# Attention output of the first batch repeated and added on TensorE, with a re-planned order of casts, copies and pooled V

## The chip, the core and the metric

The kernel runs on one core of one Trainium2 chip. The metric is the device time of one execution in microseconds (us); lower is better. Before the change the median of four runs is 338.2 us (336.63 to 339.19).

## What is computed

Two steps in one launch: an "hourglass" attention on q, k, v of shape (8 batches, 8 heads, 576 tokens, 64), and a feed-forward on its output.

```python
q_d, k_d, v_d = (mean over groups of 4 tokens)       # 144 tokens
out_d  = softmax(q_d @ k_d.T / 8) @ v_d
out_up = np.repeat(out_d, 4, axis=2)                 # back to 576 tokens
local  = softmax over |i - j| < 4 of q @ k.T / 8, times v
x = (out_up + local).transpose(0, 2, 1, 3).reshape(4608, 512)
h = x @ w_in                                         # (512, 2048)
out = (h - np.tanh(h)) @ w_out                       # (2048, 512), float32
```

## The kernel before, in words

**Pairs and groups.** The unit of attention is a pair of heads of one batch (`attention(p)`, 32 pairs, p = 0 to 31, four to a batch); q and k are loaded and turned for two pairs at a time (group n = p // 2). The unit of the dense part is a block of 512 tokens (kb, nine of them): 16 steps of `mm1` (h of 128 features: four matmuls L739, tanh on ACT L748, subtraction to gT on DVE L751), then `mm2` (gT times w_out, L794, copied out by ACT L805). One batch is 576 tokens, so block 0 can begin once all four pairs of batch 0 are in xT: each mm1 step reads xT of all four.

**A group on its way in.** DMA brings q and k to `qkn` (L372). `reorder` casts them to bf16 `qr` (L477). `turn` transposes on TensorE (nine transposes, L505, into a PSUM tile) and copies to `qk` (L514). Two additions make the pooled q and k (L518 to `half`, L523 to `qkd`). V comes to `vst` (L398) and is cast to `vw` (L435); `pool_v` pools V of a group with six matmuls by a 0/1 matrix `pick` (L453, L455) and ACT copies it to `vd` (L460).

**A pair.** Local scores come in 120-column tiles: s1 (L572) and s2 (L572 and, for the pooled scores, L591). In batch 0 the mask is added in PSUM first by a matmul with the identity (L566). ACT takes the exps to E (L608, L634, L637); later batches multiply by the mask on DVE (L612, L641). `outs` makes both outputs with their sums (L652 local, L658 pooled). DVE takes reciprocals (L669) and normalises to `ln` (L671). For p < 12 TensorE transposes `ln` back: two transposes of the pooled part (L706, L707) and five of the local part (L710), all bf16 into PSUM. ACT copies the pooled part to `od` (L713), and DVE adds local and repeated pooled part into xT (L715). From p = 12 on a DMA transposes `ln` to `lnT` and DVE adds (L691).

**PSUM.** `ps_ts` and `ps_ox` serve attention. While batch 0 is in the works, the even pairs have a second set, `ps_ts1` and `ps_ox1`; these banks become the four `ps_hy` of the dense part.

**Order.** Nothing runs in the order of the code. Each `op` is recorded with an engine, a cost, its reads, writes and a priority; `choice` leaves the engine open. `Program.order()` lays all of them out by a list schedule, and `emit` issues them in that order, so each engine's queue is fixed when the kernel is built. In it come the constants near the end: which engine casts what (`CV`, `RE`, `TU`, `AD`, `CAST`), which copies and additions are split in two halves (`TS`, `AS`), in which PSUM set a group is turned (`TB`), where a group's turning and V pooling is placed (`PLACE`, `PV`), priorities (`LATE`, `URG`), margins between engines (`LATER`, `SPARE`), how far loads run ahead (`AHEAD`), and the order of the weight loads (`ORDER`: g is the load of the next group, 0 to 3 are quarters of w_out). SyncE (SP) issues all DMAs in one queue: q, k, v of batch 0, the four quarters of w_in, group 2, then group 3 and w_out. Weights are staged as float32 and cast (L426).

**Fillers.** Where the plan shows TensorE idle for over 350 ns before the first dense step, `emit` puts in matmuls of a zero tile `warm` (L1006), as many as 0.75 of the gap divided by an assumed duration (`slow`).

Of the kernel before, what the change touches and what calls it, by code (L numbers as in the profile page):

```python
# [9 lines left out]
BF16 = mybir.dt.bfloat16  # L10
AF = mybir.ActivationFunctionType
ALU = mybir.AluOpType
# [3 lines left out]
class Program:  # L16
# [127 lines left out]
    def emit(self, banks=None, end=None, filler=None):  # L144
        order = self.order()
        fill = {}
        if filler:
            until = min(self.start[i] for i in range(len(self.ops)) if end in self.touch[i])
            self.uses = {name: sorted(
                (self.start[i], self.start[i] + self.ops[i][1] + 200, i in self.fresh)  # L150
                for i in range(len(self.ops)) if self.touch[i] & set(keys))
                for name, keys in banks.items()}
            for i, name, room in self.idle(order, banks, until):
                slow = 430 if self.start[i] < 6000 else 230
                fill[i] = (name, int(0.75 * room / slow))
        for i in order:
            if i in fill:
                filler(*fill[i])
            if self.ops[i][2] is not None:
                self.ops[i][2]()  # L160
# [3 lines left out]
def kernel(  # L164
# [10 lines left out]
    B, H, S, D = q.shape  # L175
# [10 lines left out]
    QW = 120  # L186
    NT = 5
# [22 lines left out]
    warm = fixed("warm", [128, 512], BF16)  # L210
# [40 lines left out]
    P = Program()  # L251
# [6 lines left out]
    LATER = 160  # L258
# [29 lines left out]
    def c_bias():  # L288
# [3 lines left out]
        for part, pat in ((m4, [[0, 4], [1, QW]]),  # L292
# [13 lines left out]
            fill=OFF, base=99, pattern=[[0, 96]], channel_multiplier=-1)  # L306

# [50 lines left out]
    def load_qk(n):  # L358

        b, h0, s = n // 2, 4 * (n % 2), slot_qk(n)  # L360
        for i, src in enumerate((q, k)):
            P.put(n, ("qkn", s, i))
            for y in range(2):
# [7 lines left out]
                def issue(to=to, rows=rows):  # L371
                    nc.sync.dma_start(out=to, in_=rows)  # L372
                load(650, issue, [("qkn", s, i, y)],
                     T_QK + (400 if n == 0 and i == 1 else 0), -30,
# [66 lines left out]
    def pool_v(hb):  # L441
# [6 lines left out]
        bank, key = (ps_ox1, "ox1") if hb == 0 else (ps_ox, "ox")  # L448
        pv = bank[:, 0, :].rearrange("p (w c) -> p w c", w=2)

        def mm():
# [8 lines left out]
        op("ACT", 600, lambda: A.copy(  # L460
            out=vd[w][:, :, :, 0:64],
            in_=pv.rearrange("p w (h d) -> p w h d", d=D)),
# [8 lines left out]
    def reorder(n, i):  # L471
        s, sn = n % 2, slot_qk(n)
        P.has(n, ("qkn", sn, i))
        P.put(n, ("qr", s, i))
        dst = qr[s][:, i].rearrange("p a (x d) -> p x a d", d=D)
        srt = qkn[sn][:, i].rearrange("p x (a d) -> p x a d", d=D)
        P.choice([(eng, ns, lambda fn=fn: fn(out=dst, in_=srt))  # L477
                  for eng, ns, fn in REORDER[RE.get((n, i), 3 + i)]],
                 reads=[("qkn", sn, i, x) for x in range(2)],
                 writes=[("qr", s, i)], pri=20 * n - 12)  # L480

    def turn(n, i):
# [7 lines left out]
        pri, cold = 20 * n, (1.5 if n < 1 else 1.0)  # L490
        b16 = ps.rearrange("p n c -> p (n c)").bitcast(BF16)[:, 0:A6 * 128]
        if n >= FI:
# [6 lines left out]
               reads=[("qr", s, i)], writes=ts + [("q", ("qT", i))], pri=pri - 60)  # L499
            op("DMA", T_IN, None, reads=[("q", ("qT", i)), ("qr", s, i)], writes=ts,  # L500
# [5 lines left out]
        if n < FI:  # L506
            P.fresh.add(len(P.ops))
            op("PE", 480 * cold, tr, reads=[("qr", s, i), "ident"], writes=ts, pri=pri)
# [40 lines left out]
    def attention(p):  # L549
# [97 lines left out]

        def outs():
# [29 lines left out]

        if p >= XOUT:
# [6 lines left out]
            xo = xT[j][:, b * S:(b + 1) * S]  # L686
# [14 lines left out]


# [23 lines left out]
    def mm1(kb, fc):  # L726
# [15 lines left out]
        for part in range(2):  # L742
# [3 lines left out]
               [("x", b, j) for b in bs for j in dcs],  # L746
# [66 lines left out]
    def dense(kb):  # L813
# [18 lines left out]
        if kb == NBLK:  # L832
# [4 lines left out]
    XOUT, T_OUT, AHEAD = 12, 1600, 6  # L837
    P_A, LATE = 5000, {0: 26, 1: 5, 2: 25, 3: 25}
    MERGE, GV = 12, 7
    FI, T_IN = 11, 2050  # L840
    XADD = [("DVE", (800, 350), V)]
    ORDER, W_FIRST = 'g0123', '0123qv'
    TB = {(1, 0), (1, 1), (2, 0), (3, 0)}
    PV = {2: -1, 3: 0, 4: 1, 5: 0, 6: 0}
    PLACE = {2: (2, 4), 3: (1, 3), 4: (4, 4), 5: (0, 2), 6: (2, 3), 7: (1, 1), 8: (0, 3)}
    W_LATE = [300, 1400, 0, 0]
    T_QK, T_V, T_W, W_PRI = 900, 780, 2750, 33
# [5 lines left out]
    CV = {0: 0, 1: 0, 2: 3, 3: 1, 4: 1, 5: 0, 6: 0, 7: 3, 8: 1, 9: 0, 10: 2, 11: 1}  # L853
# [4 lines left out]
    RE = {(0, 0): 4, (0, 1): 4, (1, 0): 4, (1, 1): 4, (2, 0): 1, (2, 1): 0, (3, 0): 3, (3,  # L858
          1): 4, (4, 0): 3, (4, 1): 4, (5, 0): 1, (5, 1): 1}
# [3 lines left out]
    TU = {(0, 0): 0, (0, 1): 0, (1, 0): 1, (1, 1): 0, (2, 0): 0, (2, 1): 0, (3, 0): 0, (3,  # L863
          1): 0, (4, 0): 2, (4, 1): 1, (5, 0): 2, (5, 1): 0}
# [6 lines left out]
    TS, AS = {(0, 0): 1, (1, 1): 3, (4, 0): 3}, {(0, 1): 3, (1, 1): 3}  # L871
    URG = {'e1': {4: -2, 5: -2, 6: -2, 7: -2}, 'od': {4: -2, 5: -2, 6: -2, 7: -2}, 'norm':
          {8: -2, 9: -2, 10: -2, 11: -2}, 'add': {4: -2, 5: -2, 6: -2, 7: -2}, 'turn': {4:
          -2, 5: -2}}
    ADDERS = [[("DVE", 760, 440, V), ("POOL", 1190, 850, GP)],
              [("POOL", 1190, 880, GP)], [("DVE", 760, 440, V)]]
    AD = {(0, 0): 0, (0, 1): 1, (1, 0): 0, (1, 1): 2, (2, 0): 1, (2, 1): 0, (3, 0): 0, (3,
          1): 0, (4, 0): 1, (4, 1): 0, (5, 0): 0, (5, 1): 2}
# [5 lines left out]
    op("POOL", 500, c_mask, reads=["bias"], writes=["mask"], pri=20)  # L884
# [82 lines left out]
    for hb in range(2):  # L967
        pool_v(hb)
    for p in range(NPAIR):
# [14 lines left out]
        if p % 2 == 0 and 1 < n < GV and PV.get(n, 0) == 1:  # L984
            pool_v(n)
        next(work[p], None)
# [17 lines left out]
    def filler(name, n):  # L1004
        for _ in range(n):
            T.matmul(tiles[name][:, 0, :], warm[:, 0:128], warm, start=True, stop=True)  # L1006
# [31 lines left out]
```

## Time and profile before

The profiled execution took 339.19 us, of which 337.5 us are the span from first to last instruction; it is the slowest of the four.

| what | us |
|---|---|
| TensorE busy, of 337.5 | 319.7 |
| DVE, ACT, POOL busy | 238.3, 207.6, 149.1 |
| first dense matmul (L739) | 27.16 |
| dense matmuls without a break from | 30.49 |
| first mm2 matmul (L794) | 51.88 |
| mean granted TensorE clock, 0 to 20, 20 to 30, 30 to 40, 40 to 50 us | 1.00, 0.81, 0.68, 1.00 |
| last matmul ends | 334.5 |

Lines of the timeline give start, length, engine, source line, operation, output and inputs with shapes, how many in a row, and in brackets the idle time before and what ended it. PE is TensorE, SPq the DMA-issuing queue of SyncE. In rows of windows a number in brackets counts instructions. The granted clock is a share of full speed. Durations of matmuls include their passage through the array; what counts in a row of matmuls is their distance.

### The profile page before, as it was taken

The numbers are of one execution on the slowest core, as the hardware profiler recorded it, in microseconds if no ns is written. First come the engines' busy times: TensorE is split into PE (matmuls) and PEld (weight loads), VectorE is DVE, ScalarE is ACT, GpSimd is POOL, SyncE is SP. The second block draws the span as 40 slices with busy tenths as digits, with TensorE's granted clock in tenths as the row PEclk, the third lists the DMA queues.
The fourth block names the chain that finished last, engine by engine and source line by source line (L and its number), as shares of the span: only waits on it lengthen the run. The fifth ranks groups of instructions, "written<-read, shape, count | busy, mean of one in ns | idle before, by whom it ended". The sixth has DMA issues, their size and how long they took to land.

```text
span 337.5 us, 6713 instructions
## 1 busy us (share of the span) xinstructions
PE 319.7 (95%) x2522; PEld 165.5 (49%) x2565; DVE 238.3 (71%) x385; ACT 207.6 (62%) x337; POOL 149.1 (44%) x168
## 2 busy tenths in 40 slices
PE   6687999999999999999999999999999999999996
PEld 2363445555555555545444545444444444444444
DVE  3986799789996898799787887898665443343300
ACT  2574688558777767485959794958754344344421
POOL 8642196187389268986664776473200000000000
PEclk9995899999999999999999999999999999999999
DMA  6999999899920599999999999993124100100012
GB/s 199 248 383 321 281 337 325 226 291 231 316 74 33 105 234 271 223 256 206 252 220 242 211 270 228 254 223 83 63 61 79 40 33 31 62 33 32 31 65 94
DMA packets 96878, 60.47 MB, mean 179 GB/s; under 512 B 74510, under 2 KB 80078, under 8 KB 96846
## 3 DMA queue, kind: packets, MB, share of 16 engines
q1 hardware_dynamic: 96846, 60.04, 70.0%
q8 instruction: 20, 0.33, 0.4%
q14 instruction: 12, 0.10, 0.1%
HBM read 43.05 MB, written 9.44 MB: 156 GB/s over the span
## 4 chain that ended last, share of the span: by engine, by line
PE 80%; DVE 8%; DMA 4%; SPq 2%; issue 2%; ACT 1%; POOL 1%; ACTq 0%; POOLq 0%; DVEq 0%
PE ps_hy L739 34%; PE ps_hy L794 33%; PE ps_ox L652 3%; PE ps_ts L572 2%; DMA gT<-in_moe_w_in_dram 2%; DVE gT L751 2%; PE ps_ox L658 2%; PE ps_ts L505 2%; SPq L398 2%; DMA qkn<-in_k_dram 2%; DVE xT L715 1%; DVE ln L671 1%; PE ps_hy L769 1%; ACT uy L748 1%; POOL half L518 1%
## 5 line engine op out<-in xcount | busy, mean ns | idle before, releaser
L739 PE MATMUL ps_hy<-xT,w_in_sb 128*128 128x512 bf16 x549 | 144.9, 386 | 4.6 <-DVE xT L715 2.2
L751 DVE TENSOR_TENSOR gT<-ps_hy,uy 128x512 bf16<-128x512 f32 x144 | 95.3, 684 | 62.3 <-ACT uy L748 61.7
L794 PE MATMUL ps_hy<-w_out_sb,gT 128*128 128x512 bf16 x545 | 137.4, 379 | 0.8 <-issue 0.2
L748 ACT ACTIVATE uy<-ps_hy 128x512 f32<-128x512 f32 x144 | 83.3, 604 | 58.1 <-PE ps_hy L739 54.6
L739 PEld LDWEIGHTS <-w_in_sb 128*128 128x128 bf16 x576 | 54.0, 99 | 63.7 <-issue 7.4
L794 PEld LDWEIGHTS <-gT 128*128 128x128 bf16 x560 | 52.6, 98 | 59.1
L518 POOL TENSOR_TENSOR half<-qk 128x576 f32<-128x576 bf16 x26 | 32.2, 1237 | 50.5 <-ACT qk L514 42.7
L671 DVE TENSOR_TENSOR ln<-ps_ox,r 128x896 bf16<-128x896 f32 x30 | 32.7, 1090 | 0.9
L608 ACT ACTIVATE E<-ps_ts 128x960 bf16<-128x960 f32 x30 | 29.5, 986 | 2.8 <-PE ps_ts L572 2.8
L805 ACT COPY uy<-ps_hy 128x512 f32<-128x512 f32 x35 | 20.9, 596 | 14.9 <-PE ps_hy L794 13.2
L435 POOL CAST vw<-vst 128x640 bf16<-128x640 f32 x28 | 24.3, 868 | 7.6 <-PE ps_ox L652 3.8
L348 POOL TENSOR_TENSOR qkn<-qkn 128x512 f32<-128x512 f32 (+1 forms) x18 | 23.1, 1284 | 9.4 <-DMA qkn<-in_v_dram 8.7
L612 DVE TENSOR_TENSOR E<-E,mask 128x960 bf16<-128x960 bf16 x28 | 25.0, 892 | 1.6 <-ACT E L608 1.5
L691 DVE TENSOR_TENSOR xT<-lnT 128x480 bf16<-128x480 bf16 (+1 forms) x40 | 25.7, 655 | 0.0
L477 POOL CAST qr<-qkn 128x1152 bf16<-128x1152 f32 x17 | 20.7, 1218 | 10.5 <-DMA qkn<-in_k_dram 10.1
L514 ACT COPY qk<-ps_ts 128x1152 bf16<-128x1152 bf16 (+1 forms) x15 | 15.9, 1062 | 13.9 <-DVE qk L514 8.0
L514 ACT COPY qk<-vst 128x1152 bf16<-128x1152 bf16 x10 | 22.2, 2222 | 1.5 <-POOL half L518 1.5
L523 POOL TENSOR_TENSOR qkd<-half 128x288 bf16<-128x288 f32 x28 | 21.4, 764 | 2.6 <-DVE half L518 1.3
L652 PEld LDWEIGHTS <-E 128*128 128x128 bf16 x300 | 15.4, 98 | 7.3 <-DVE E L641 0.6
L652 PE MATMUL ps_ox<-vw,E 128*128 128x65 bf16 x300 | 18.4, 194 | 0.6 <-DVE E L641 0.4
L634 ACT ACTIVATE E<-ps_ox 128x192 bf16<-128x192 f32 x20 | 6.7, 333 | 18.7 <-PE ps_ox L591 18.7
L572 PEld LDWEIGHTS <-qk 64*128 64x128 bf16 x320 | 9.4, 95 | 17.0 <-issue 13.8
(97 smaller groups left out, 290.6 us busy)
## 6 DMA issues: line engine op xcount, KB each, us to landing
vst<-in_v_dram SPq DMA_DIRECT2D x62, 160.0 KB, 4.9
qkn<-in_q_dram SPq DMA_DIRECT2D x32, 288.0 KB, 4.3
qkn<-in_k_dram SPq DMA_DIRECT2D x32, 288.0 KB, 5.0
out_dram<-uy SPq DMA_DIRECT2D x35, 256.0 KB, 3.8
qkn<-in_v_dram SPq DMA_DIRECT2D x9, 512.0 KB, 5.2
gT<-in_moe_w_in_dram SPq DMA_DIRECT2D x4, 1024.0 KB, 10.2
xT<-in_moe_w_out_dram SPq DMA_DIRECT2D x8, 256.0 KB, 4.7
gT<-in_moe_w_out_dram SPq DMA_DIRECT2D x2, 1024.0 KB, 10.7
```

What stands on the lines that cost most here:

```text
L435: P.choice([(eng, ns, lambda fn=fn: fn(out=vw[w][:, 2 * jj:2 * jj + 2, :, 0:64], in_=vst[s])) for eng, ns, fn in CAST_V[CV.get(p, 1)]], re ...
L514: fn(out=o[:, ys].rearrange("p y (g a) -> p y g a", a=A6), in_=b16.rearrange("p (a g y) -> p y g a", a=A6, y=2)[:, ys])
L518: eng.tensor_tensor(out=half[:, ys], in0=four[:, ys, :, 0:2], in1=four[:, ys, :, 2:4], op=ALU.add)
L608: op("ACT", 980, lambda: A.activation(out=e1, in_=ps[:, :, 0:480], func=AF.Exp, scale=SCALE), reads=ts, writes=[("E", se, 0)], pri=URG.get ...
L612: op("DVE", 900, lambda: V.tensor_tensor(out=e1, in0=e1, in1=mask[:, 0:480].unsqueeze(1).to_broadcast([128, 2, 480]), op=ALU.mult), reads= ...
L652: T.matmul(po[:, hh, 65 * t:65 * t + 65], E[se][:, c:c + 128], vw[w][:, 2 * jj + hh, t, :], start=True, stop=True)
L671: op("DVE", 1090, lambda: V.tensor_tensor(out=ln[sl].rearrange("p n (h d) -> p h n d", d=D), in0=blocks[:, :, :, 0:64], in1=r[s].unsqueeze ...
L691: up=up: eng.tensor_tensor(out=xo[:, QW * t0:QW * t0 + nt * n].rearrange("p (t g a) -> p t g a", t=nt, a=4), in0=lnT[sl][:, t0:t0 + nt, 0: ...
L739: T.matmul(ps_hy[slot], w_in_sb[:, dc, fc * 128:(fc + 1) * 128], xT[dc][:, kb * 512:kb * 512 + 512], start=(dc == 0), stop=(dc == N_DC - 1))
L748: op("ACT", 490, lambda: A.activation(out=u[us], in_=ps_hy[slot], func=AF.Tanh), reads=[("hy", slot)], writes=[("u", us)], pri=-1)
L751: op("DVE", 620, lambda: V.tensor_tensor(out=gT[g][:, fc, :], in0=ps_hy[slot], in1=u[us], op=ALU.subtract), reads=[("hy", slot), ("u", us) ...
L794: T.matmul(ps_hy[slot], gT[g][:, fc, ts * 128:ts * 128 + 128], w_out_sb[:, fc, :], start=(fc == 0), stop=(fc == N_FF - 1))
```

## The change

Output of the pairs in `UP` (0 to 4, 8 and 11) is no longer transposed back in bf16 and added by DVE. TensorE multiplies `ln` with 0/1 matrices in float32 PSUM: the pooled part by `spread`, which repeats each pooled column four times, then the local part by the identity on top. What is left is one copy to xT, by ACT or DVE, or by both in halves (value 3). Pooled V of pairs 2-3 is made in `ps_ts1`, behind the scores of those pairs, and copied by DVE. Casts of q and k may be split in two halves (`RS`): k of group 0 by DVE and ACT, q of group 1 by ACT and POOL, k of group 1 by any. q of group 0 is left to any engine, and DVE gets it. `warm` has 320 columns instead of 512, and the assumed filler durations are shorter. The constants above are set anew; in the queue of SyncE the first quarter of w_out comes ahead of group 3. The dense part is unchanged but for the added dependence on the halves of x.

```diff
-                slow = 430 if self.start[i] < 6000 else 230
+                slow = 270 if self.start[i] < 6000 else 144
...
-    warm = fixed("warm", [128, 512], BF16)
+    warm = fixed("warm", [128, 320], BF16)
+    spread = fixed("spread", [128, 2, 288], BF16)
...
-    LATER = 160
+    LATER = 180
...
+    def c_up():
+        for i in range(2):
+            part = spread[:, i].rearrange("p (g a) -> p g a", a=4)
+            GP.memset(spread[:, i], 0.0)
+            GP.affine_select(out=part, in_=part, compare_op=ALU.not_equal, fill=1.0,
+                             base=-56 * i, pattern=[[-1, 72], [0, 4]], channel_multiplier=1)
...
-        bank, key = (ps_ox1, "ox1") if hb == 0 else (ps_ox, "ox")
+        bank, key = ((ps_ox1, "ox1") if hb == 0 else
+                     (ps_ts1, "ts1") if hb == 1 and PV1 else (ps_ox, "ox"))
...
-        op("ACT", 600, lambda: A.copy(
-            out=vd[w][:, :, :, 0:64],
-            in_=pv.rearrange("p w (h d) -> p w h d", d=D)),
+        P.choice([(eng, ns, lambda fn=fn: fn(
+            out=vd[w][:, :, :, 0:64], in_=pv.rearrange("p w (h d) -> p w h d", d=D)))
+                  for eng, ns, fn in POOLED[VD.get(hb, 1)]],
...
+        parted = RS.get((n, i), 0)
+        parts = [(x, x + 1) for x in range(2)] if parted else [(0, 2)]
+        for m, (x0, x1) in enumerate(parts):
+            table = (REORDER_H[parted - 1][m] if parted else
+                     REORDER[RE.get((n, i), 3 + i)])
...
+        if p in UP:
+            def whole():
+                for i in range(2):
+                    T.matmul(po[:, i, 0:288], ln[sl][:, 5 + i, :], spread[:, i, :],
+                             start=True, stop=False)
+                    for t in (range(3), range(2, NT))[i]:
+                        n, c = NQ[t], QW * t
+                        c0, c1 = max(c, 288 * i), min(c + n, 288 * i + 288)
+                        T.matmul(po[:, i, c0 - 288 * i:c1 - 288 * i], ln[sl][0:n, t, :],
+                                 ident[0:n, c0 - c:c1 - c], start=False, stop=c1 == 288 * i + 288)
+            op("PE", 650 * cold, whole, reads=[("ln", sl), "up"], writes=ox, pri=late)
+            parted = UP[p] == 3
+            for m, (i0, i1) in enumerate([(0, 1), (1, 2)] if parted else [(0, 2)]):
+                table = (UP_H[m] if parted else [UP_COPY, UP_COPY[:1], UP_COPY[1:]][UP[p]])
+                P.choice([(eng, ns, lambda fn=fn, i0=i0, i1=i1: fn(
+                    out=xo.rearrange("p (i c) -> p i c", i=2)[:, i0:i1],
+                    in_=po[:, i0:i1, 0:288])) for eng, ns, fn in table],
+                         reads=ox, writes=[(("x", "xh")[m], b, j)],
+                         pri=URG.get("add", {}).get(p, late))
+            return
...
-    XOUT, T_OUT, AHEAD = 12, 1600, 6
-    P_A, LATE = 5000, {0: 26, 1: 5, 2: 25, 3: 25}
-    MERGE, GV = 12, 7
+    XOUT, T_OUT, AHEAD = 12, 1600, 7
+    P_A, LATE = 5000, {0: 25, 2: 40, 3: 40}
+    MERGE, GV = 14, 7
...
-    ORDER, W_FIRST = 'g0123', '0123qv'
+    ORDER, W_FIRST = '0g123', '0123qv'
...
-    RE = {(0, 0): 4, (0, 1): 4, (1, 0): 4, (1, 1): 4, (2, 0): 1, (2, 1): 0, (3, 0): 3, (3,
-          1): 4, (4, 0): 3, (4, 1): 4, (5, 0): 1, (5, 1): 1}
+    RE = {(0, 0): 0, (0, 1): 0, (1, 0): 1, (1, 1): 1, (2, 0): 1, (2, 1): 0, (3, 0): 3, (3,
+          1): 0, (4, 0): 2, (4, 1): 1, (5, 0): 0, (5, 1): 0}
...
+    PV1 = True
+    VD = {0: 1, 1: 2, 2: 1, 3: 0, 4: 1, 5: 0, 6: 1}
+    RS = {(0, 1): 2, (1, 0): 4, (1, 1): 1}
+    UP = {0: 0, 1: 0, 2: 0, 3: 3, 4: 3, 8: 0, 11: 3}
...
-    TS, AS = {(0, 0): 1, (1, 1): 3, (4, 0): 3}, {(0, 1): 3, (1, 1): 3}
+    TS = {(0, 0): 1, (0, 1): 2, (1, 1): 2, (2, 1): 2, (4, 0): 2, (5, 0): 2, (5, 1): 1}
+    AS = {(1, 0): 2, (1, 1): 1, (2, 0): 1, (2, 1): 1, (5, 0): 1, (5, 1): 4, (6, 1): 1}
...
-            T.matmul(tiles[name][:, 0, :], warm[:, 0:128], warm, start=True, stop=True)
+            T.matmul(tiles[name][:, 0, 0:320], warm[:, 0:128], warm, start=True, stop=True)
```

`CV`, `TU`, `AD`, `PV`, `PLACE`, `TB`, `URG`, `T_QK`, `W_LATE` and `W_PRI` are set anew in the same way.

## The prediction

> **What bounds the kernel now.** I read the engine shares and the clock row first, then the chain of work that ended last, then windows and the timeline of the first 40 us, because the first view says where to look.
>
> ```profile
> PE 319.7 (95%) x2522; PEld 165.5 (49%) x2565; DVE 238.3 (71%) x385; ACT 207.6 (62%) x337; POOL 149.1 (44%) x168
> PEclk9995899999999999999999999999999999999999
> PE 80%; DVE 8%; DMA 4%; SPq 2%; issue 2%; ACT 1%; POOL 1%; ACTq 0%; POOLq 0%; DVEq 0%
> ```
>
> TensorE is busy 95% of the span and 80% of the chain. From about 30 us to the last matmul at 334.5 it is the bound, so time can come from three places only: an earlier start of the dense stage, faster matmuls in it, fewer waits in it. The clock row has one dent, slices of 8.44 us at 25 to 42 us. Windows of 3.4 us (columns: stretch, length, busy PE, PEld, DVE, ACT, POOL, granted clock, DMA share, GB/s) show its edges:
>
> ```profile
> 5.50:8.90 3.40, 1.56 (x14) 0.91 (x14) 1.01 (x2) 0.64 (x1) 3.08 (x3) 1.00 0.94 287
> ...
> 22.80:26.20 3.40, 1.84 (x38) 1.41 (x34) 3.37 (x5) 2.11 (x6) 1.30 (x3) 1.00 1.04 387
> 26.20:29.60 3.40, 1.91 (x9) 1.11 (x10) 2.57 (x6) 1.21 (x4) 0.73 (x2) 0.50 1.06 390
> 29.60:33.00 3.40, 2.51 (x6) 0.86 (x6) 2.12 (x4) 1.34 (x4) 0.77 (x2) 0.50 1.06 258
> 33.00:36.40 3.40, 3.40 (x9) 1.22 (x8) 1.86 (x3) 1.18 (x3) 1.59 (x2) 0.50 0.96 272
> 36.40:39.80 3.40, 3.40 (x31) 2.08 (x29) 2.26 (x4) 2.36 (x4) 0.00 (x0) 1.00 0.99 263
> ```
>
> The clock is exactly half from 26.2 to 36.4. DVE is busy 3.37 of 3.40 just before: it is what the end of the ramp waits for. The timeline of that end:
>
> ```profile
> 24.93 1.41 DVE L715 TENSOR_TENSOR xT<-ps_ox,od 128x576 bf16<-128x576 bf16 x2
> ...
> 27.02 1.08 DVE L671 TENSOR_TENSOR ln<-ps_ts,r 128x896 bf16<-128x896 f32 x1
> 27.16 0.59 PE L739 MATMUL ps_hy<-xT,w_in_sb 128*128 128x512 bf16 x1 [0.98 <-DVE xT L715]
> ...
> 29.37 0.28 ACT L713 COPY od<-ps_ts 128x144 bf16<-128x144 bf16 x1 [2.00 <-PE ps_ts L710]
> 29.68 0.76 DVE L715 TENSOR_TENSOR xT<-ps_ts,od 128x576 bf16<-128x576 bf16 x1 [0.92 <-ACT od L713]
> 30.49 8.03 PE L739 MATMUL ps_hy<-xT,w_in_sb 128*128 128x512 bf16 x23 [1.21 <-DVE xT L715]
> ```
>
> Pair 3 is normalised (27.02 to 28.10), transposed back, copied (od), added, and at 30.49 the fourth matmul of the first dense group can go. The 23 matmuls then take 8.03 us; at the 0.216 us apart of the full-clock rows (8 in 1.73 us) they would take 5.1 with the last one's drain.
>
> **The change, part by part.** I walk the built order of the changed kernel with durations of this trace. Pairs are numbered 0 to 3.
>
> *Head of TensorE's queue.* 29 fillers of 320 columns replace 9 of 512. At half clock a 512-column filler takes 0.427 us, so 320 take 0.267; at full clock 0.135. The trace has fillers at half clock until at least 4.65 and normal transposes at 6.47; I take 5.5 for the lift. Then 16 fillers are slow, 13 fast, and they end at 1.24 + 4.26 + 1.8 = 7.3. q of group 0, now cast by DVE (0.75), is ready near 6.0, so its transposes go at 7.3, not 6.47: 0.8 late. All 29 slow would be 9.0, a lift at 4.65 gives 6.9.
>
> *k cast by two engines.* k of group 0 lands at 8.24 (chain). POOL cast it 8.37 to 9.51. Now DVE takes half (0.4) but ACT's half (0.6) stands behind its qk copy (8.8 to 9.45), so it ends at 10.05; the bias matmuls and five fillers stand ahead of the transposes too: 10.55, not 9.57. This edit by itself loses about 1 us.
>
> *What pays it back.* DVE did the first pooled adds itself (half 1.47, qkd 1.28, 8.65 to 11.43) and copied k only at 11.36 to 12.71. They are on POOL now, freed of four casts of 1.14 to 1.23 us but for two halves. The halves of the k copy follow one another (each waits for the other engine), but pair 0 needs the first alone: 11.27 + 0.64 = 11.9, scores at 11.95 instead of 12.77. From there ACT sets the pace with the rows 0.99 (L608), 0.34 + 0.65 (L634, L637): E of pair 0 starts at 12.55, of pair 1 at 13.6, their later parts at 14.8 and 16.5 (a qk half of 0.64 between), E of pair 2 at 17.5 instead of 18.74, vd at 18.55, E of pair 3 at 19.2 instead of 21.43: its scores stood behind the pooling of V of pairs 2-3, which now follows them (in ps_ts1).
>
> *End of the ramp.* The outputs of pairs 1 and 0 wait for vd (19.15); the first is ready at 20.15. Then DVE holds: four reciprocals and normalisations of 0.24 + 1.09 = 5.3, the vd copy (0.65, estimated from the 0.59 of ACT's L460 and DVE's 0.76 for a 576-column L514), xT of pair 0 (0.72, same neighbours), hand-overs 0.2: 27.1. The w_in casts that stood between (L426 at 21.28, 1.18) are on POOL and ACT. Pair 3's repeat and add: 2 x 288 + 576 = 1152 columns, 0.48 us at full clock (512 in 0.216) plus 0.17 drain: 27.8. ACT's half copy 0.37, then DVE's half, which waits for it, 0.41: 28.7. The od copy and the od-dependent add are gone from this path. Three matmuls of the first group have gone by then in both kernels: 30.49 to 28.7 is **1.8 us gained**. Ends: 0.6 (a late clock lift, or POOL slowing DVE) to 2.8.
>
> *The clock.* Here a rule speaks against the change. The Trainium skill (TensorE: Matmul & The Clock Gate, Why this matters for your kernels) has TensorE keep its clock as long as no idle gap between bursts exceeds about 3 us. The longest gap near the drop is 0.98 us, so by the rule fillers and fuller windows buy nothing, and the 2.9 us of the half clock would stay: the sum below would end at 337.8. The rows disagree: the clock did fall with 1.84 us busy out of 3.4, while 5.5 to 8.9 with 1.56 busy did not make it fall. The same page (Part 4: PE-mode transpose) says that transposes do not count as busy like matmuls; in 22.8 to 26.2 the work was two rounds of transposes, two small score sets and 18 matmuls of 65 columns, in 5.5 to 8.9 three 512-column fillers. The change turns exactly these transposes (L706 to L710) into ordinary matmuls, and puts 5 and 2 fillers between: its poorest window, about 25.4 to 28.8, has 2.0 us of ordinary matmuls. I take the row: clock stays full, **2.9 us gained** (8.03 - 5.1). Ends: 0 and 2.9.
>
> *Dense stage.* Repeat and add for pairs 4, 8 and 11: 1152 columns for the 832 of the transposes, 0.13 us each: **+0.4**. DVE can follow: summed over both orders with the page's means it has 1.9 us less to do before the first gT and 1.9 less at the 64th, and it idled 4.1 us in 30 to 40 us because TensorE was slow there.
>
> *w_out.* TensorE reaches the second dense stage some 4.7 us earlier (51.9 to about 47), but transfers do not come earlier:
>
> ```profile
> gT<-in_moe_w_out_dram SPq DMA_DIRECT2D x2, 1024.0 KB, 10.7
> 43.12 1.14 SPq L419 DMA_DIRECT2D gT<-in_moe_w_out_dram x2
> ```
>
> The last two quarters land at 53.8 and 54.4. Before, they were wanted at 63.3; now, by the built order (16 matmuls on quarter 0, two outputs' work, then quarters 1 and 2), at about 54.3, with casts done at 54.7 and 57.5. **+0.5**, from 0 to 2.
>
> *All else* (constants that move casts between engines, loads one pair earlier, merged scores from pair 14, POOL's spread constant 1.4 us before the mask, hidden since POOL no longer casts q first). TensorE idles 2.6 us in 60 to 180, so at most 1.5 to win; up to 2 to lose if an order fits worse. I take 0.
>
> Sum: -1.8 - 2.9 + 0.4 + 0.5 = -3.8 against the profiled execution's 339.19: 335.4. That execution is the slowest of four, 1.0 above the median; its excess is either the clock dent (then 335.4 stands) or something the change keeps (then 334.4). Middle: **334.9**.
>
> **Rivals.** *A, likeliest, 0.56*: as summed; own range 333.5 to 336.3. *B, the clock falls again, 0.12*: the gap rule or a window that falls badly; 334.9 + 2.9 = 337.8, no change that can be told. For it: 60% busy is no safe distance. *C, TensorE stands on w_out or DVE, 0.15*: 2 us more of waiting at 54 to 58 us or while DVE is at 95% (28.54 of 30 in 70 to 100): 336.9. *D, the new order also removes waits after 60 us and the ramp gains its 2.8, 0.12*: 332.7. *E, slower, 0.05*: q of group 3 now lies behind a quarter of w_out, and its cast stands on DVE with all gT steps queued behind it. Four issues of 0.43 and 1 MB at about 0.33 MB/us put its landing near 39 to 40; DVE gets to the cast near 41.8. Each us beyond that is a us; slower than before by 0.5% from a landing at about 47.5: 340.5. Against it: the transfers fell to 146 GB/s at 32 to 33 us, room that w_out fills.
>
> **Numbers.** 0.5% (1.7 us) is about what a measurement tells from no change. Faster than 336.5: A's 0.56 nearly whole, D, half of C: 0.76. Within: the rest of C, B: 0.18. Slower: 0.06, E with a little of B. The range 332.6 to 337.3 reaches from D's time past C and leaves out B, E and what lies under D.
>
> **What would show it.** First full dense run at 28.2 to 29.2; granted clock 1.00 in all windows from 6 to 40; the first 24 dense matmuls over by 33.5 (38 before); mm2 starting near 47; waits on L426 w_out casts under 1 us. The head is right if q's first transposes start near 7.3 and k's near 10.5. Wrong if the clock row has its dent again, if DVE waits on q of group 3, or if the dense stage from 60 us takes longer than before.

## The result, and the profile after

| | before | changed |
|---|---|---|
| median of the runs | 337.89 us (60 runs, 334.3 to 341.63) | 335.58 us (39 runs, 334.22 to 337.27) |
| profiled execution | 339.19 us, span 337.5, granted clock 0.984 | 334.75 us, span 333.0, granted clock 1.00 |

The ratio is 0.9959, with a 95% interval from 0.9941 to 0.9976: 1.4 us faster, where the prediction had 3.3 (334.9 against the 338.2 that was the median of the runs shown). This ratio leaves out the executions of the kernel before that lie over 1.5% above its fastest (14 of 60), so it is nearer to 1 than the ratio of the medians in the table, 0.993 (2.3 us).

The changed kernel's page, to set beside the lines of before: engine shares, clock row, chain by engine.

```profile
PE 320.1 (96%) x2563; PEld 168.7 (51%) x2606; DVE 234.7 (70%) x386; ACT 209.7 (63%) x338; POOL 154.9 (47%) x183
PEclk9999999999999999999999999999999999999999
PE 88%; DVE 6%; issue 3%; ACT 1%; POOL 1%; DVEq 0%; ACTq 0%; POOLq 0%
```

The dent at 25 to 42 us is gone; TensorE's busy time is what it was, and its share of the chain grew from 80% to 88%. The 3.4 us windows over the place of the dent (columns: stretch, length, busy PE, PEld, DVE, ACT, POOL, clock, DMA share, GB/s):

```profile
22.80:26.20 3.40, 2.87 (x58) 2.46 (x56) 3.16 (x5) 2.35 (x5) 1.28 (x3) 1.00 1.04 386
26.20:29.60 3.40, 2.57 (x23) 1.34 (x22) 2.83 (x7) 1.55 (x3) 1.33 (x3) 1.00 1.05 386
29.60:33.00 3.40, 3.28 (x16) 1.50 (x16) 2.40 (x5) 2.47 (x5) 1.17 (x2) 1.00 1.02 218
```

TensorE is busy 2.87 where it was 1.84, and the clock stays. TensorE's timeline at the end of the ramp:

```profile
28.58 0.81 PE L777 MATMUL ps_hy<-xT,w_in_sb 128*128 128x512 bf16 x2
29.72 4.69 PE L777 MATMUL ps_hy<-xT,w_in_sb 128*128 128x512 bf16 x21 [0.33 <-DVE xT L734]
```

The full dense run starts at 29.72, against 30.49 before and 28.7 predicted, and its first 21 matmuls take 4.69 us where 23 took 8.03. So from profile to profile it is 4.4 us, more than predicted, and from all runs to all runs 2.3, about half of that. The experiments are about this contradiction. "Ramp" stands for the time up to the full dense run.

### The profile page after: what moved, and what is told of

It is laid out like the page before. It is cut to its first block, busy times and chain, and to the rows that moved or that the text cites. A ratio compares the mean times of both kernels' runs of the same rounds, so it can differ in the third digit from the quotient of the medians.

```text
span 333.0 us, 6822 instructions
## 1 busy us (share of the span) xinstructions
PE 320.1 (96%) x2563; PEld 168.7 (51%) x2606; DVE 234.7 (70%) x386; ACT 209.7 (63%) x338; POOL 154.9 (47%) x183
## 4 chain that ended last, share of the span: by engine, by line
PE 88%; DVE 6%; issue 3%; ACT 1%; POOL 1%; DVEq 0%; ACTq 0%; POOLq 0%
PE ps_hy L777 36%; PE ps_hy L832 34%; PE ps_ts L587 3%; PE ps_ox L669 3%; PE ps_ts L520 2%; PE ps_ts L1064 2%; PE ps_ox L675 2%; DVE ln L688 1%; DVE qk L529 1%; PE ps_hy L807 1%; ACT qk L529 1%; PE ps_ox L520 1%; PE ps_ox L462 1%; PE ps_ox L606 1%; DVE E L656 1%
## 5 line engine op out<-in xcount | busy, mean ns | idle before, releaser
L777 PE MATMUL ps_hy<-xT,w_in_sb 128*128 128x512 bf16 x553 | 141.8, 379 | 2.2 <-issue 1.1
L777 PEld LDWEIGHTS <-w_in_sb 128*128 128x128 bf16 x576 | 53.1, 98 | 59.3 <-issue 1.0
L533 POOL TENSOR_TENSOR half<-qk 128x576 f32<-128x576 bf16 (+1 forms) x33 | 34.8, 1058 | 44.2 <-ACT qk L529 37.9
L443 POOL CAST vw<-vst 128x640 bf16<-128x640 f32 x27 | 25.0, 932 | 7.9 <-DMA vst<-in_v_dram 7.4
L708 DVE TENSOR_TENSOR xT<-lnT 128x480 bf16<-128x480 bf16 (+1 forms) x40 | 27.0, 691 | 0.0
L356 POOL TENSOR_TENSOR qkn<-qkn 128x512 f32<-128x512 f32 (+1 forms) x18 | 25.7, 1428 | 1.9 <-DMA qkn<-in_v_dram 1.2
L627 DVE TENSOR_TENSOR E<-E,mask 128x960 bf16<-128x960 bf16 x28 | 22.7, 812 | 5.1 <-ACT E L623 5.1
L538 POOL TENSOR_TENSOR qkd<-half 128x288 bf16<-128x288 f32 (+1 forms) x31 | 20.4, 661 | 5.8 <-DVE half L533 4.6
L491 DVE CAST qr<-qkn 128x1152 bf16<-128x1152 f32 (+1 forms) x18 | 18.0, 1000 | 2.7 <-DMA qkn<-in_q_dram 2.7
L491 POOL CAST qr<-qkn 128x1152 bf16<-128x1152 f32 (+1 forms) x14 | 16.2, 1161 | 6.1 <-DMA qkn<-in_k_dram 5.9
```

Source lines behind the costliest of these rows:

```text
L356: op("POOL", 1330, lambda t=t: GP.tensor_tensor(out=t[:, :, 0:2], in0=t[:, :, 0:2], in1=t[:, :, 2:4], op=ALU.add), writes=keys, pri=pri)
L491: P.choice([(eng, ns, lambda fn=fn, x0=x0, x1=x1: fn(out=dst[:, x0:x1], in_=srt[:, x0:x1])) for eng, ns, fn in table], reads=[("qkn", sn, ...
L533: eng.tensor_tensor(out=half[:, ys], in0=four[:, ys, :, 0:2], in1=four[:, ys, :, 2:4], op=ALU.add)
L708: up=up: eng.tensor_tensor(out=xo[:, QW * t0:QW * t0 + nt * n].rearrange("p (t g a) -> p t g a", t=nt, a=4), in0=lnT[sl][:, t0:t0 + nt, 0: ...
L777: T.matmul(ps_hy[slot], w_in_sb[:, dc, fc * 128:(fc + 1) * 128], xT[dc][:, kb * 512:kb * 512 + 512], start=(dc == 0), stop=(dc == N_DC - 1))
```

## Experiments

**Theory M (mixture):** the clock drop at 26 to 36 us is in a part of the executions of the kernel before only; an execution without it is as fast as the changed kernel, whose whole effect is that it never drops. **Rival R:** the drop is in all executions, and the change gives back later what it gains. **Rival R2:** beside the clock, the shorter ramp is worth something of its own.

**1. The kernel before once more, with the clock of each execution.** No edit.

> The kernel before once more, unchanged, to see the granted clock of each of its executions beside its time. Theory M (mixture): the half clock at 26 to 36 us is there in a part of the executions only; runs with a mean clock of 0.98 to 0.99 take 337 to 341 us, runs with 0.997 or more take 334.3 to 336, as long as the changed kernel, and nothing lies between. Rival R (always): the half clock is in every execution (mean clock 0.98 to 0.99 in all), and the spread from 334 to 341 us comes from somewhere else, such as transfers; then the change gains 2.9 us on the clock and gives some 1.5 us back in the dense stage.

Measured: 338.33 us, 333.9 to 339.74. The profiled execution is not like the one of before: the clock row of its page has two shallow dips side by side instead of one deep one.

```profile
PEclk9978999999999999999999999999999999999999
```

The mean clock of a run lies near one of a few values, 1.00, 0.995, 0.99, 0.985 and 0.98, that is zero to four stretches of 3.41 us at half clock in some 337 us (each 0.5%). All 155 executions of the kernel before that have a clock beside their time:

| mean clock | executions | median us | range |
|---|---|---|---|
| 0.997 or more | 33 (21%) | 335.0 | 333.9 to 337.2 |
| 0.992 to 0.996 | 15 (10%) | 336.0 | 335.3 to 337.7 |
| 0.987 to 0.991 | 73 (47%) | 338.0 | 335.8 to 340.3 |
| under 0.987 | 34 (22%) | 339.5 | 337.9 to 343.4 |

One stretch at half clock costs up to 1.7 us (half of 3.41), and medians 1.0, 3.0 and 4.5 us above the first row fit one, two and three. (A fourth adds nothing: the 13 runs at 0.98 or less have the median 339.3.) M holds, except that "nothing lies between" was wrong: there are four groups, not two. R falls: a fifth of the executions never drop, and they take 335.0 us. The profiled execution of the prediction (0.984, three stretches) belongs to the slowest fifth.

The windows of this second profile, cut where its clock changes:

```profile
13.87:17.28 3.41, 1.65 (x22) 0.94 (x21) 3.10 (x6) 2.92 (x6) 1.72 (x4) 1.00 1.07 255
17.28:20.69 3.41, 3.39 (x18) 1.62 (x18) 2.10 (x5) 1.72 (x3) 0.86 (x1) 0.50 1.05 393
...
24.10:27.51 3.41, 2.04 (x42) 1.54 (x39) 3.34 (x7) 2.13 (x6) 1.17 (x2) 1.00 1.05 387
27.51:30.92 3.41, 1.77 (x25) 1.01 (x23) 3.09 (x7) 1.65 (x5) 0.79 (x2) 1.00 1.13 360
30.92:34.33 3.41, 2.62 (x7) 0.97 (x7) 2.10 (x4) 1.35 (x3) 0.72 (x2) 0.50 0.43 93
```

The clock falls at 17.28 and 30.92 and rises 3.41 later, on one grid: (34.33 - 17.28) / 5 = 3.41. The stretch ahead of each fall has 1.65 and 1.77 us of busy TensorE, the one between, which is kept, 2.04. In the first profile the grid lay otherwise (26.20, 22.79), with 1.85 ahead of the fall. So the clock of the same program falls, or doesn't, by where the stretches cut it. This is the free-running window of the Trainium skill (TensorE: Matmul & The Clock Gate, Part 1: What's actually happening), which it puts at 3413 ns; these traces agree.

**2. The kernel before, kept warm.** 21 matmuls on the zero tile, where TensorE waits anyway.

```diff
+    def keep(to, n):
+        for _ in range(n):
+            T.matmul(to, warm[:, 0:128], warm[:, 0:to.shape[-1]], start=True, stop=True)
         def s2():
...
+            if p == 3:
+                keep(sc[:, 384:512], 14)
         def back():
...
+            if p == 0:
+                keep(po[:, 1, 256:512], 2)
         def mm(part):
...
+            if kb == 0 and fc == 0 and part == 1:
+                keep(ps_hy[3], 4)
             for dc in range(cut) if part == 0 else range(cut, N_DC):
...
+            if kb == 0 and fc == 0 and part == 0:
+                keep(ps_hy[3], 1)
```

> The kernel before plus 21 matmuls on the zero tile at the end of the ramp, put where TensorE waits anyway (14 of 128 columns behind the scores of pair 3, 2 of 256 behind the transposes of pair 0, 5 of 512 around those of pair 3); nothing else is changed. Theory M: the half clock is gone (mean clock 0.997 or more in all runs), the time is 335.0 to 335.8 us and its spread 3 us as in the changed kernel, so that the repeat on TensorE, the two-engine k cast and the moved pooling bring nothing beside it; the dense run starts at 29.7, not 30.5. Rival R2: the ramp of the change is worth its 0.8 to 1.8 us beside the clock; then this kernel stays 0.8 to 1.8 us above the changed one, 336.4 to 337.4. Should the clock still fall, lack of work in that stretch is not its cause.

Measured: 334.82 us (334.15 to 335.74), clock 0.995 in two of 12 runs, which lost nothing by it (334.15 and 334.64), and 1.00 in the rest. It was run twice more, first beside the changed kernel on the same chip, then beside the last experiment:

> The kernel before with the 21 keep-warm matmuls once more, now beside the changed kernel on the same chip. Theory M (the change is worth its clock and nothing else, and costs 0.4 us of repeat work and 0.2 us of ramp): 0.4 to 1.0 us below the changed kernel. Rival (the changed order has gains of its own): equal or above.

> The changed kernel once more, unchanged, as the base for the three beside it on the same chip: 335.0 to 336.0 us, clock 0.999 or 1.0 in all executions.

> The kernel before with its 21 keep-warm matmuls, beside the kernel above on the same chip, to see which of the two is the best: 334.8 to 335.2 us. Where a stretch of 3.41 us falls on its dip at 13.6 to 14.2, a mean clock of 0.995 that costs nothing, since TensorE is not what is waited for there.

Measured: 335.15 and 335.25 us; the changed kernel on the chip of the first of these 335.66 (ratio of medians 0.9985, interval by resampling 0.9964 to 1.0002). All 36 runs of the kept-warm kernel have the median 335.15, all 52 of the changed kernel 335.58: ratio 0.9987, interval 0.9978 to 0.9997, over different chips. The ramp's end in its trace:

```profile
28.16 1.03 PE L551 MATMUL ps_hy<-warm 128*128 128x512 bf16 x4
29.52 5.12 PE L749 MATMUL ps_hy<-xT,w_in_sb 128*128 128x512 bf16 x23 [0.34 <-DVE xT L723]
```

With its clock kept, the old order starts its dense run at 29.52 (29.82 and 29.97 in the other two profiles); the changed one at 29.72 (30.07 in its second profile). R2 falls: 21 matmuls that compute nothing bring all that the change brings, and seem 0.4 us better; on one and the same chip the interval still includes no difference. No version with the full output was measurably faster.

**3. Which part of the change holds the clock?** First the new fillers alone in the kernel before, then the changed kernel without its last seven.

```diff
-                slow = 430 if self.start[i] < 6000 else 230
+                slow = 270 if self.start[i] < 6000 else 144
...
-    warm = fixed("warm", [128, 512], BF16)
+    warm = fixed("warm", [128, 320], BF16)
```

> The kernel before with the changed kernel's filler rule alone: 27 fillers of 320 columns (13, 5 and 5 ahead of 12 us, 2 and 2 ahead of 20 us) for 15 of 512. Theory M: the window that decides lies at 22.8 to 26.2 us, where no filler is added, so the half clock comes as often as before: 337.5 to 338.2 us, spread 7 us. Rival: the fillers, not the ordinary matmuls, are what keeps the clock: 335.3 us, clock 0.997 or more. The longer head can cost up to 0.8 us in either case.

```diff
-                fill[i] = (name, int(0.75 * room / slow))
+                fill[i] = (name, int(0.75 * room / slow) if self.start[i] < 15000 else 0)
```

> The changed kernel without its last 7 fillers (the 5 and 2 that stand between the outputs of the first pairs). By the transposes' account (ordinary matmuls in their place keep the clock up) the clock stays at 0.997 or more and the time at 335.6 us. By the busy-time account (what counts is how much of a 3.4 us window is busy) about 1 us of work is missing from the poorest window, and a part of the runs gets the half clock again: mean clock 0.985 to 0.99 in these, 338 us, the median between 335.6 and 338.

Measured: 339.22 us for the first, with 10 of 12 runs at 0.979 to 0.99; 335.51 for the second, clock 0.999 or 1.00 in all 12. Fillers at the head do nothing for a drop at 25 us, and the late ones weren't needed: the new order holds the clock without them, though without the seven some stretches of its trace (starts of 24.8 to 26.2) have only 1.83 to 1.9 us busy. The profiled execution of the first happened not to drop, and it too starts its dense run at 29.52.

**4. Do transposes count?** The kept-warm kernel, its added work as transposes.

```diff
-        for _ in range(n):
-            T.matmul(to, warm[:, 0:128], warm[:, 0:to.shape[-1]], start=True, stop=True)
+        for _ in range(n * to.shape[-1] // 128):
+            T.transpose(to.bitcast(BF16)[:, 0:128], warm[:, 0:128], ident)
```

> The kernel before kept warm as in the second experiment, but the added work is transposes of the zero tile in the same places and of the same number of columns (14 + 4 + 20 of 128 columns) in place of ordinary matmuls. If transposes do not count as busy for the clock, which is what the Trainium skill says of them (TensorE: Matmul & The Clock Gate, Part 4: PE-mode transpose) and what the prediction leaned on, the half clock comes back in about three runs of four: median 337.5 to 338.2, clocks of 0.98 to 0.99. If any streamed column counts, all runs stay at 0.995 or more and the time at 334.8 us.

Measured: 336.06 us (334.37 to 337.79); nine of 12 runs at 0.999 or 1.00, three at 0.994 to 0.995 (336.9 to 337.8); of the kernel before on that chip 4 of 27 runs were at 1.00, one at 0.995 and 22 at 0.99 or less. Transposes keep the clock nearly as well as matmuls. That they don't count, on which the prediction leaned, falls: here the measurement decides, against the page. The profile of before says the same: its stretch of 9.11 to 12.52 kept the clock with 2.12 us of busy TensorE, 1.35 of it transposes (L505), while in experiment 1 the stretch of 13.87 to 17.28 fell with 1.65, nearly all of it ordinary matmuls. That they count a little less stays open.

**5. Half of the keep-warm work,** without the five matmuls around pair 3's transposes.

```diff
-            if kb == 0 and fc == 0 and part == 1:
-                keep(ps_hy[3], 4)
-            if kb == 0 and fc == 0 and part == 0:
-                keep(ps_hy[3], 1)
```

> The kernel before with only the first 16 of the 21 keep-warm matmuls (14 behind the scores of pair 3, 2 behind pair 0's transposes), none around pair 3's transposes. Account by windows: TensorE's busy time in a stretch of 3.41 us decides, the stretches lie anywhere relative to the program, and under some 1.87 us the clock is halved for the next stretch. In an undropped trace of the kernel before, stretches that start at 22.8 to 24.4 and at 25.2 to 26.7 lie under that; the 16 matmuls lift the first of these to 2.0 or more and leave the second, 1.6 of 3.41 us: 40 to 50% of the executions should show a mean clock of 0.991 or less, against 70% in the kernel before and 0% with all 21. If instead the first dip alone starts the drop, none should.

Measured: 336.67 us, beside 336.99 of the kernel before on that chip; three of 12 at 0.99, two at 0.995. Its profiled run is one of those that fell, at 27.63:

```profile
20.81:24.22 3.41, 3.14 (x69) 2.75 (x69) 2.64 (x6) 2.01 (x6) 1.62 (x2) 1.00 1.05 390
24.22:27.63 3.41, 1.69 (x33) 1.41 (x34) 3.38 (x7) 2.67 (x7) 1.73 (x3) 1.00 1.05 388
27.63:31.04 3.41, 1.99 (x10) 1.12 (x10) 2.61 (x6) 0.83 (x3) 0.67 (x2) 0.50 1.10 358
```

The first dip is filled: a stretch from 22.80 has 2.40 us in this trace, and 1.84 in the trace of before. The second dip (1.69) let the clock fall. So 42% of the runs fell at all and 25% for two stretches or more, where 40 to 50% were expected for the latter; the kernel before falls in 79%, the fully kept-warm one in 6 of 36, each for one stretch. The account by windows fits in direction; 12 runs don't prove its number.

**6. Single parts of the change taken back, the rest planned anew.** Transposes back; k of group 0 by one engine; pooled V of pairs 2 and 3 as before.

```diff
-    UP = {0: 0, 1: 0, 2: 0, 3: 3, 4: 3, 8: 0, 11: 3}
+    UP = {}
...
-    RS = {(0, 1): 2, (1, 0): 4, (1, 1): 1}
+    RS = {(1, 0): 4, (1, 1): 1}
...
-    PV1 = True
+    PV1 = False
```

> The changed kernel without the repeat and add on TensorE: transposes, od copy and DVE's add as before, no spread constant; the rest of the change stays, though the order shifts with it. Theory M says that this part brings nothing in the ramp beside the clock and costs 0.4 us of TensorE time later: 335.0 to 335.4 where the clock holds (0.2 to 0.6 below the changed kernel's 335.6). If the repeat is what shortens the ramp, as the prediction had it, this kernel is 1 to 2 us slower, 336.6 to 337.6, at a clock of 0.997 or more. If the repeat's ordinary matmuls hold the clock, the half clock comes back in a part of the runs: 338, clock 0.98 to 0.99.

> The changed kernel with k of group 0 cast by one engine instead of DVE and ACT by halves. The prediction had this edit by itself at a loss of about 1 us at k's transposes, but hidden behind what frees DVE; then the time stays within 0.4 us of 335.6. If the early pairs set the end of the ramp, it moves by up to 1 us either way: 334.6 or 336.6.

> The changed kernel with the pooling of V of pairs 2 and 3 in its old bank and old place in the order, ahead of the scores of pair 3. The prediction counted this as the reason that E of pair 3 starts 2 us earlier. If it is, the ramp ends 1 to 2 us later: 336.6 to 337.6 at a clock of 0.997 or more. Theory M (the ramp's end is set by DVE's reciprocals, normalisations and copies, in both orders) has it within 0.4 us: 335.2 to 336.0.

Measured: 340.49, 343.09 and 335.49 us. The first two are misses that say little of the parts: the planner put the whole rest of the program in another order. Their ramps end near the changed one's (dense runs from 30.17 and 29.23), but the dense stage has new stalls. TensorE's waits at 98 to 122 us of the first (columns: line and what was waited for, us in total, times, longest):

```profile
PE ps_ox L462 <- DVE xT L753: 1.2, 1, 1.2
PE ps_ts L587 <- ACT qk L529: 1.2, 1, 1.2
```

and from 100 to 120 us TensorE is busy 16.70 of 20 us and its clock falls once more (0.91 there, 0.994 over the run). The third kept the rest nearly in place: 335.49, dense run from 30.05. Pooling V elsewhere brings nothing in the time, and no ramp beyond the spread of the changed kernel's own two profiles (29.72 and 30.07).

**7. The repeat on TensorE by itself.** Pairs 3, 4 and 11 transposed back, copied and added as before, in the place of the new instructions, the order untouched.

```diff
             def whole():
+                if old:
+                    T.transpose(px[1][:, 0:128], ln[sl][:, 5, :], ident)
+                    T.transpose(px[1][:, 16:144], ln[sl][:, 6, :], ident)
...
+                if old:
+                    def back(fn, m=m):
+                        if m == 0:
+                            A.copy(out=od[s], in_=px[1][:, 0:144])
+                        else:
+                            V.tensor_tensor(
...
```

> The changed kernel with pairs 3, 4 and 11 transposed back in the old way (transposes, od copied by ACT, DVE's add of 576 columns) in exactly the changed order: the same instructions stand everywhere else. This is the repeat by itself, which the run with all transposes back could not show, since its order shifted. In the ramp DVE's half of 0.46 becomes an add of 0.76, the transposes take 0.17 us less of TensorE than the repeat: the dense run starts 0 to 0.3 later. In the dense stage TensorE has 2 x 0.13 us less, DVE 2 x 0.3 more. Theory M: within 0.4 us of the changed kernel. If the repeat carries the ramp's gain as the prediction had it, 1 us or more above; if it is what holds the clock, runs of 0.98 to 0.99 appear.

Measured: 335.84 us against 335.66 of the changed kernel beside it, dense run from 29.83, one of 12 runs at 0.995. At pair 3 the repeat carries neither the ramp nor the clock; pairs 0 to 2 were not tried by themselves.

**8. A shorter head.** 18 fillers for 29 ahead of q's transposes.

```diff
-                fill[i] = (name, int(0.75 * room / slow))
+                n = int(0.75 * room / slow)
+                fill[i] = (name, n if n < 20 else 18)
```

> The changed kernel with 18 fillers ahead of q's first transposes for 29; the order is otherwise the same. The prediction put q's transposes 0.8 us later than before because of the fillers, and traced 7.46 against 6.47. Without 11 of them they should go near 6.4. If the head passes on to the end of the ramp, the dense run starts 0.4 to 0.8 earlier and the kernel takes 334.8 to 335.2; if k's arrival at 8.24 and DVE hold the ramp, nothing moves: within 0.2 us of the changed kernel. Should the clock fall in the head for lack of fillers, it costs 0 to 1.7 us.

Measured: 335.52 us, beside 335.66. q's transposes start at 6.33 and k's at 9.62 (7.46 and 10.74 in the changed kernel), but the dense run at 29.66 (29.72). A microsecond won at the head is gone by 15 us, where k of group 1 is transposed at 15.03 against 15.10.

**9. Why is the ramp 1 us longer than the prediction's walk?** DVE and POOL in the changed kernel, and a wait of TensorE:

```profile
16.36 0.77 POOL L533 TENSOR_TENSOR half<-qk 128x288 f32<-128x288 bf16 x1 [3.26 <-DVE qk L529]
16.53 0.92 DVE L533 TENSOR_TENSOR half<-qk 128x288 f32<-128x288 bf16 x1
17.37 0.75 DVE L529 COPY qk<-ps_ox 128x576 bf16<-128x576 bf16 x1
17.99 0.42 POOL L538 TENSOR_TENSOR qkd<-half 128x144 bf16<-128x144 f32 x1
18.04 0.54 DVE L538 TENSOR_TENSOR qkd<-half 128x144 bf16<-128x144 f32 x1
18.49 0.66 POOL L533 TENSOR_TENSOR half<-qk 128x288 f32<-128x288 bf16 x1
18.61 0.86 DVE L533 TENSOR_TENSOR half<-qk 128x288 f32<-128x288 bf16 x1
...
20.27 0.30 PE L606 MATMUL ps_ts<-qkd 64*128 64x144 bf16 x4 [0.29 <-DVE qkd L538]
```

DVE's adds of 288 columns take 0.92 and 0.86 us; the planner's own cost for one is 0.42. The pooled scores at 20.27 wait for DVE's last add, and the outputs of the first pairs stand behind them, at 20.50. POOL has three such adds at 16.36 to 19.15. In the experiment these three cover 4 columns, so the output of pairs 2 and 3 lacks part of its pooled scores:

```diff
         def add1(eng, ys):
+            if n == 1 and eng is GP:
+                GP.tensor_tensor(out=half[:, ys, 0:4], in0=four[:, ys, 0:4, 0:2],
+                                 in1=four[:, ys, 0:4, 2:4], op=ALU.add)
+                return
```

> The changed kernel, but POOL's three adds for the pooled q and k of pairs 2 and 3 (0.77 + 0.42 + 0.66 us at 16.4 to 19.1) cover 4 columns instead of 288 and 144; the rest of their result is zeros, so the output of these pairs is not the reference's. All else is in the changed order. If these adds on POOL are what made the ramp 1 us longer than the prediction's walk (DVE's own adds took 0.86 to 0.92 and 0.46 to 0.54 beside them, 0.46 and 0.31 with POOL idle; POOL's V cast stands behind them), DVE's adds fall to 0.46 and 0.31, the outputs of pairs 1 and 0 start near 19.6 instead of 20.5, and the dense run starts 0.7 to 1.0 earlier, 28.7 to 29.0: 334.6 to 334.9 us. If DVE's normalisations of pairs 2 and 3 or the exponentials set the end anyway, the start stays at 29.4 to 30.1 and the time at 335.6.

DVE and POOL there:

```profile
16.57 0.46 DVE L537 TENSOR_TENSOR half<-qk 128x288 f32<-128x288 bf16 x1
16.66 0.94 POOL L443 CAST vw<-vst 128x640 bf16<-128x640 f32 x1
16.95 0.75 DVE L529 COPY qk<-ps_ox 128x576 bf16<-128x576 bf16 x1
17.62 0.30 DVE L546 TENSOR_TENSOR qkd<-half 128x144 bf16<-128x144 f32 x1
17.95 0.46 DVE L537 TENSOR_TENSOR half<-qk 128x288 f32<-128x288 bf16 x1
17.99 1.00 POOL L443 CAST vw<-vst 128x640 bf16<-128x640 f32 x1
```

The same adds take 0.46, while the copy from PSUM between them takes 0.75 in both. The outputs start at 19.61 instead of 20.50, the dense run at 28.85, and the time is 334.55 us: the walk's 28.7 would have been nearly right had these three adds on POOL cost DVE nothing.

POOL is not idle in these rows: its casts run beside both adds, but they start after them. That is the difference. In the rows of the changed kernel POOL's add is under way when DVE's starts, and DVE's ends 0.32 us after POOL's (17.13 and 17.45, 19.15 and 19.47). It holds for all of DVE's adds of 288 columns in the traces of this case: of 28 that started with no POOL operation under way none took over 0.46 us, though in 18 POOL started one meanwhile; 47 started during a POOL operation and ended 0.30 to 0.42 after it.

Then the same with all work kept, and POOL's adds only moved behind its V casts:

```diff
         order = self.order()
+        late = {113: 18300, 114: 18310, 120: 18320, 121: 19990}
+        order = sorted(order, key=lambda i: (late.get(i, self.start[i]), i))
```

> The changed kernel, its whole computation, with POOL's three pooled adds of pairs 2 and 3 moved behind its two V casts, and the one DVE add that reads them moved behind DVE's first normalisation; nothing else moves. If POOL's adds beside DVE's cost the ramp 1 us, as the run with those adds cut showed, but where they stand is what matters and not that they run, DVE's adds now fall to 0.46 and 0.31, the V cast goes 0.7 earlier, and the dense run starts 0.6 to 1.0 earlier, 28.8 to 29.3, for 334.6 to 335.0 us. If the slowdown only moves to the next DVE step beside the adds (the normalisation), or pair 3's pooled scores come late, the start stays at 29.5 to 30.1 and the time at 335.6.

Measured: 336.20 us, dense run from 29.95: a miss.

```profile
16.25 1.01 POOL L445 CAST vw<-vst 128x640 bf16<-128x640 f32 x1 [0.68 <-DMA vst<-in_v_dram]
16.59 0.97 DVE L535 TENSOR_TENSOR half<-qk 128x288 f32<-128x288 bf16 x1
...
18.15 0.29 DVE L540 TENSOR_TENSOR qkd<-half 128x144 bf16<-128x144 f32 x1
18.16 0.56 POOL L540 TENSOR_TENSOR qkd<-half 128x144 bf16<-128x144 f32 x1
```

DVE's first add now starts during the V cast and takes 0.97; the add at 18.15 starts just ahead of POOL's and takes 0.29. So a cast on POOL holds DVE's add up as much as an add does, and what counts is whether POOL's operation is already under way. The outputs do start earlier (20.02), but TensorE waits 1.22 us at 22.77 for the one DVE add that was moved. Whether a better place for POOL's adds saves the 0.9 us stays open.

## Why the prediction was off

- **What bounds the kernel: half right.** The dense stage from 30 us and the dent were read rightly. But "that execution is the slowest of four" was taken for an excess of 1 us that might or might not be the dent; it was three stretches of half clock, 4.5 us, and 22% of the executions have three or four, while 21% have none. The four times shown already spread over 2.6 us.
- **The clock, -2.9: the step that failed.** The mechanism is right: a stretch with 1.84 us busy lets the clock fall against the rule of gaps (the gap of 0.98 us even lies behind the fall; the longest in the stretch is 0.80), and in none of the changed kernel's 52 executions does it fall. The size is wrong, since the term was read from one execution and taken from all: against executions that never drop it is 0, and against the runs that the ratio compares (median 336.9) some 2 us. Counted over all 155 executions (median 337.5, undropped 335.0) it is 2.5, so the whole effect of the change is this one term. The row on transposes was explained wrongly (experiment 4).
- **End of the ramp, -1.8: failed, measured 0.** Two halves of about 1 us. The 30.49 that it was counted from held the drop itself: undropped, the old order starts at 29.5 to 30.0. And the walk let the outputs of pair 1 wait for vd alone (ready at 20.15); they stood behind scores that waited for DVE's adds, which POOL's held up, and were ready at 21.2 (experiment 9). The trace of before had both cases: 0.46 and 0.75 for an add of 288 columns, and the 1.47 and 1.28 that the prediction counts as DVE's own for the first adds contain such waits, since each started during a cast on POOL (adds of their size took 0.76 and 0.46 on DVE in the changed kernel).
- **The head: right.** q's and k's transposes at 7.46 and 10.74 (7.3 and 10.55 predicted), scores at 12.19 (11.95), vd at 18.95 (18.55). The spread constant took POOL 3.0 us and not 1.4; no effect of it shows. Experiment 8 shows that the 0.8 charged here costs nothing.
- **Repeat, +0.4:** not seen by itself (experiment 7 took pairs 3, 4 and 11 out and was 0.2 us slower, within the scatter of its runs). But the changed kernel is 0.17% (0.04 to 0.23 by resampling), 0.6 us, above the undropped executions of before (over several chips), about this term and the 0.2 of ramp; that split is argued, not shown.
- **w_out, +0.5: not there.** The first matmul of the second dense stage starts at 46.4 (47 predicted), and TensorE waits 0.3 us in all from 40 to 60 us, none of it for w_out. q of group 3 is cast at 41.78, the foreseen 41.8; rival E did not happen, nor B or C.
- The time itself, 335.58, lies in the range, and the sum's 335.4 is close to it, but by luck: the profiled execution had lost 4.5 us to its clock, and the two gains of 2.9 and 1.8, the second for another reason, add up to about that. From the right base (335.0, without a drop) the terms come to 0 + 0 + 0.4 + 0.

## What to carry to other kernels

A single profile is one execution. Before a dent in its clock row is priced, ask how many executions have it: the mean clock beside each time tells, and so does a spread of the times that is several times what the kernel usually shows. If the dent comes from a thin stretch of TensorE, try first to put idle matmuls where TensorE waits anyway; a rebuilt order must then be measured against that, and not against the dented run. And an add moved to POOL is not free for DVE beside it: a DVE add that starts during POOL's operation ends only after it, so ask which of the two will start first.

## What the runs showed of the hardware

- The granted clock changes on a grid of 3.41 us whose place relative to the program differs between executions. Of all stretches on that grid that the traces of this case show at full clock, seven were followed by a fall. They had 1.56 to 1.89 us of busy TensorE, and no gap in them was longer than 1.49 us. No stretch with more than 1.89 fell, but six with 1.68 to 1.85 were kept. So low busy time is needed for a fall and does not settle it; what exactly is counted stays open. Two stretches of one trace, experiment 4's, show it: the first was kept, the second led to the fall (which came at 27.69, so that the window here lies 0.04 early; on the grid itself it has 1.89):

```profile
14.01:17.42 3.41, 1.75 (x26) 1.20 (x26) 3.10 (x6) 3.06 (x6) 2.04 (x3) 1.00 1.02 229
24.24:27.65 3.41, 1.93 (x38) 1.51 (x35) 3.38 (x7) 2.36 (x7) 1.18 (x2) 1.00 1.06 389
```

- Half clock is not always kept for one stretch: after a stretch at half clock with 1.91, 1.99, 2.03 and 2.53 us busy it stayed, after 2.62 and more it rose.
- Of the six runs of the kept-warm kernel with one stretch at half clock two were among its fastest (334.15 and 334.64 us) and one its slowest (337.39). Its thinnest stretch is at 13.6 us in its first profile (1.78 us busy), but at 24.0 and 24.4 in the other two (1.69 and 1.64). So 21 matmuls do not save the clock wherever the grid falls; where these six fell was not traced.
- DVE's adds of 288 columns (bf16 in, float32 out) took 0.46 us where they started before any operation of POOL, and 0.86 to 0.97 in experiment 9 where POOL's add or cast was under way; its copy of 576 columns out of PSUM took 0.75 in both.
